# Half-height transpositions and a swapped order of projections in a linear-attention step

## The chip, the cores and the metric

The kernel runs on one core of one Trainium2 chip. The metric is the device time of one execution in microseconds (us). The engines are called as in the profile: PE is the matrix engine (PEld its weight loads), DVE, ACT and POOL are the vector, scalar and GpSimd engines, SP issues DMAs.

## What is computed

Three layers follow one another. The first is a linear attention over 8 batches, 8 heads, 576 positions and a head dimension of 64:

```python
def phi(x):
    proj = np.einsum('bhsd,df->bhsf', x, w_phi)
    proj = proj - np.max(np.abs(proj), axis=-1, keepdims=True)
    return np.concatenate([np.exp(proj), np.exp(-proj)], axis=-1)
q_p, k_p = (phi(q), phi(k))
kv = np.einsum('bhsf,bhsd->bhfd', k_p, v)
z = np.sum(k_p, axis=2)
num = np.einsum('bhsf,bhfd->bhsd', q_p, kv)
den = np.einsum('bhsf,bhf->bhs', q_p, z)[..., None] + 1e-06
```

Its output `num / den` is laid out as [batch, position, 512]. The second layer gates a 512x512 product with a causal convolution of five taps and a sigmoid and multiplies by a second 512x512 matrix. The third adds the real part of a two-dimensional Fourier transform, normalises, and adds a feed-forward block of width 2048 with ReLU. The change touches the first layer alone.

## The kernel before, in words

The attention works on 16 units (a pair of batches times a pair of heads, `NU`), and each unit has 1152 positions, in nine chunks of 128. A step takes three chunks (`CH = 3`), so that there are 48 steps (`TOT`). `run_attention` (line 1327) is a software pipeline written out by hand: turn `st` of its loop emits stages that belong to different steps, and under `manual_schedule` each engine carries them out in the order in which they are emitted. In one turn that order is:

- `emit_KV` (line 282) of step st-2: sums phi(k) times v over the positions. It uses tiles of 128 rows by 64 columns, two side by side. A step of the middle third of a unit has four pieces here and the others three, and it does two of them ahead of `emit_num`. When half a unit is summed, ACT copies the sums out (`kvT`); there is one PSUM buffer for them (`ps_kv`).
- `emit_num` (line 318) of step st-4: phi(q) times kv, in the same tiles of 128 by 64, into `nm`.
- `emit_Y` (line 264) of step st-1 for the keys (w = 0): DVE takes the largest absolute value of each row (line 268, `m`) and subtracts it (line 269, `y`). Then `emit_kE`, two exponentials on ACT. Then `emit_Y` for the queries (w = 1).
- `emit_XT` (line 343) of step st-5: three PE transpositions of 128x128 of the attention's output `xs`, into the PSUM tile that is also the keys' projection buffer (tag `pj0`). `emit_xT` (line 350): DVE copies the result out.
- `emit_X` (line 333) of step st-4: DVE divides num by den, from `nm` into `xs`.
- `emit_yT` (line 304) of step st-2: six PE transpositions of 128x128 of the queries' `y`, into the PSUM tile `tr`. `emit_qE` (line 312): two exponentials on ACT from there.
- `emit_P` (line 254) of step st, for the keys and then for the queries: projections of 64 rows by 128 columns, six for each, the two heads in the two halves of the rows. An f32 product is two instructions in the trace, so that there are 24 records for a step. The PSUM pool `ps_pj` (line 215) has one buffer for each tag, `pj0` for the keys and `pj1` for the queries.

All eight PSUM banks are taken. Between these stages the loop spreads the conversion of weights from 64 bits (`convert`, line 118: ACT lines 143, 147, 149 and POOL lines 144 to 151) and the copies of tables.

The last steps' remaining stages (`note_tail`, line 1292) and the two other layers are put in order by a planner, `place_ops`, from costs that stand in the code; the costs noted there for `emit_yT`, `emit_XT` and `emit_xT` are the same in both kernels.

Of the kernel before, what the change touches and what calls it, by code (L numbers as in the profile page):

```python
# [9 lines left out]
F32 = mybir.dt.float32  # L10
# [5 lines left out]
ACTF = mybir.ActivationFunctionType  # L16
# [5 lines left out]
NB, NH, S, D, F = 8, 8, 576, 64, 128  # L22
# [45 lines left out]
def attention_moe_mixer_kernel(  # L68
# [18 lines left out]
    nc = tc.nc  # L87
    pe, act, vec, gps = (Issue(x) for x in (nc.tensor, nc.scalar, nc.vector, nc.gpsimd))
    mm = pe.matmul

    def pool(stack, name, bufs, space=None, side=None):
        kw = {} if space is None else {"space": space}
        if side is not None:
            kw["side"] = side
        if space is not DRAM:
            kw["reuse_waits"] = "tile"
        return stack.enter_context(tc.tile_pool(name=name, bufs=bufs, **kw))
# [71 lines left out]
    ident = base.tile([128, 128], F32, name="ident")  # L169
# [22 lines left out]
    NG, CH = 3, 3  # L192
    HALVES = (slice(0, 64), slice(64, 128))
# [23 lines left out]
    qe_p = pool(att, "qe", 3)  # L217
# [14 lines left out]
    qE = {}  # L232
# [3 lines left out]
    xT = {}  # L236
# [14 lines left out]
    def chunks(t):  # L251
        return t[:, :, 0:CH * F].rearrange("p h (c f) -> p h c f", f=F)
# [11 lines left out]
    def emit_Y(i, w):  # L264
        pv = chunks(pj.pop((i, w)))
        m = sm_p.tile([128, 2, CH], F32, tag=f"m{w}", name="m")
        y = y_p.tile([128, 2, CH, F], F32, tag=f"y{w}", name="y")
        nc.vector.tensor_reduce(out=m, in_=pv, axis=AX.X, op=ALU.max, apply_absolute_value=True)  # L268
        nc.vector.tensor_tensor(out=y, in0=pv, in1=m.unsqueeze(3).to_broadcast([128, 2, CH, F]), op=ALU.subtract)  # L269
        yq[i, w] = y  # L270

    def emit_kE(i):
        y = yq.pop((i, 0))
        e = e_p.tile([128, 2, 2, CH, F], F32, tag="e", name="ke")
        nc.scalar.activation(out=e[:, 0], in_=y, func=ACTF.Exp)
        nc.scalar.activation(out=e[:, 1], in_=y, func=ACTF.Exp, scale=-1.0)
        kE[i] = e
# [4 lines left out]
    def emit_KV(i, part):  # L282
        u, g = divmod(i, NG)
        tv = raw[u][1]
        e = kE[i]
        for slot, j in KV_PARTS[g][part]:
            b = slot // 5
            if slot % 5 == 0:
                kvps[u, b] = ps_kv.tile([128, 4, 66], F32, tag="kv", name="kv")
            t = kvps[u, b]  # L290
            for h in range(2):
                for a in range(2):
                    w = 2 * h + a
                    for p in HALVES:
                        mm(t[p, w, :], e[:, a, h, j, p], tv[:, h, slot, :],
                           start=slot % 5 == 0 and w == 0, stop=slot % 5 == 4 and w == 3, skip_group_check=True)
            if slot % 5 == 4:
                if b == 0:
                    kvT[u] = sm_p.tile([128, 4, 2, 65], F32, tag="kvT", name="kvT")
                act.activation(out=kvT[u][:, :, b, :], in_=kvps.pop((u, b))[:, :, 0:65], func=ACTF.Copy)  # L300
        if part == len(KV_PARTS[g]) - 1:
            kE.pop(i)

    def emit_yT(i):
        y = yq.pop((i, 1))
        t = ps_tr.tile([128, 2, 512], F32, tag="tr", name="yt")
        for h in range(2):
            for j in range(CH):
                nc.tensor.transpose(t[:, h, j * F:(j + 1) * F], y[:, h, j, :], ident)  # L309
        yq[i, 2] = t  # L310

    def emit_qE(i, a):
        if a == 0:
            qE[i] = qe_p.tile([128, 2, 2, CH, F], F32, tag="qe", name="qe")
        t = yq[i, 2] if a == 0 else yq.pop((i, 2))
        act.activation(out=qE[i][:, a], in_=chunks(t), func=ACTF.Exp, scale=(1.0, -1.0)[a])

    def emit_num(i):
        u, g = divmod(i, NG)
        e = qE.pop(i)  # L320
        kt = kvT[u]
        nm[i] = t = ps_nm.tile([128, 2 * CH, 66], F32, tag="nm", name="nm")
        for j in range(CH):
            c = CH * g + j
            for h in range(2):
                for a in range(2):
                    for b, p in enumerate(HALVES):
                        if c != 4:
                            b = 0 if c < 4 else 1
                        mm(t[p, 2 * j + h, 0:65], e[:, a, h, j, p], kt[:, 2 * h + a, b, :],  # L330
                           start=(a == 0), stop=(a == 1))

    def emit_X(i):
# [9 lines left out]
    def emit_XT(i, space, tag):  # L343
        x = xs.pop(i)
        t = space.tile([128, 2, 512], F32, tag=tag, name="xt")
        for j in range(CH):
            nc.tensor.transpose(t[:, 0, j * F:(j + 1) * F], x[:, j].rearrange("p h d -> p (h d)"), ident)  # L347
        xs[i, 1] = t

    def emit_xT(i):  # L350
        t = xs.pop((i, 1))
        xT[i] = xT_p.tile([128, CH * F], F32, tag="xT", name="xT")
        vec.tensor_copy(out=xT[i], in_=t[:, 0, 0:CH * F])

    def x_parts(i):
        u, g = divmod(i, NG)
# [7 lines left out]
    def put_x(i):  # L364
        for b, o, k in x_parts(i):
            nc.sync.dma_start(out=o, in_=xT[i][:, k])
        xT.pop(i)
# [122 lines left out]
    def tap_steps():  # L490
        t, acc = late["xf", 0], late["sg", 0]
        act.activation(out=acc, in_=shifted(t, 0, 4), func=ACTF.Copy, scale=cw[:, 0, 4:5])
        for k in range(4):
            vec.scalar_tensor_tensor(
                out=acc, in0=shifted(t, 0, k), scalar=cw[:, 0, k:k + 1], in1=acc, op0=ALU.mult, op1=ALU.add
            )
            yield
# [829 lines left out]
    def run_attention():  # L1327
        lead = ((0, 1), (2, 0), (2, 1), (3, 0), (5, 0))
        todo = {}
        tap0 = tap_steps()  # L1330
        for i in range(len(pieces)):
            for l, slot in lead:
                todo.setdefault((i * (X_AT - 2 - lead[-1][0]) // (len(pieces) - 1) + l, slot), []).append(pieces[i])
        n_t = 2 * len(tables)
        did_t = 0
        with tc.manual_schedule():
            for st in range(TOT + 1):
                u, g = divmod(st, NG)

                def at(lag):  # L1340
                    return 0 <= st - lag < TOT

                two = at(2) and (st - 2) % NG == 1
                if two:
                    emit_KV(st - 2, 0)
                if at(4):
                    emit_num(st - 4)
                if at(6):
                    put_x(st - 6)
                if at(1):  # L1350
                    emit_Y(st - 1, 0)
                    emit_kE(st - 1)
                if at(2):
                    emit_KV(st - 2, int(two))
                for c in todo.get((st, 0), ()):
                    next(c)
                if at(1):
                    emit_Y(st - 1, 1)
                if at(5):
                    emit_XT(st - 5, ps_pj, "pj0")  # L1360
                    emit_xT(st - 5)
                if at(4):
                    emit_X(st - 4)
                if at(2):
                    emit_yT(st - 2)
                    for a in range(2):
                        emit_qE(st - 2, a)
                if at(0):
                    for w in range(2):
                        emit_P(st, w)  # L1370
                for c in todo.get((st, 1), ()):
                    next(c)
                for _ in range(2 * (TOT - 2 <= st < TOT)):
                    next(tap0)
                if g == 0 and u + 1 < NU:
                    load_kq(u + 1)
                if g == 2 and u + 1 < NU:
                    load_v(u + 1)
                while did_t < n_t and did_t * (X_AT - 5) < (st - 3) * n_t:
                    next(tables[did_t // 2])  # L1380
                    did_t += 1
                if st == X_AT:
                    assert did_t == n_t
                    load_x(0)
                    load_x(1)
                    for i in range(2):
                        late["sg", i] = P["g"].tile([128, 2, HS], F32, tag="acc", name="acc")
                if st in (X_AT + 2, X_AT + 3):
                    for i in range(2):
                        split_x(2 * (st - X_AT - 2) + i)  # L1390
            put_x(TOT - 5)
            note_mix()
            note_mlp()
            place_ops()
# [115 lines left out]
```

## Time and profile before

| | |
|---|---|
| time, median of 3 runs | 1330.14 us (1323.65 to 1333.59) |
| the profiled execution | 1323.75 us |
| its span | 1322.0 us |
| PE busy | 1288.3 us, 97% |
| PEld busy | 1186.2 us, 90% |
| DVE busy | 1151.7 us, 87% |
| ACT busy | 907.0 us, 69% |
| POOL busy | 771.1 us, 58% |

The span runs from the first to the last instruction of the program; the time holds 1.75 us more around it. Busy shares are means over stages that have different limits, so a stage is read from its own stretch of the timeline. The attention loop takes about the first 290 us. Some 41 of its 48 steps repeat one of two patterns with small differences, so one step of each stands for many.

### The profile page before, as it was taken

Reading aid. Unit: us, or ns where it says so; the run is one execution under the profiler, and the core shown is the slowest. Engines: PE = TensorE matmul, PEld = TensorE weight load, DVE = VectorE, ACT = ScalarE, POOL = GpSimd, SP = SyncE. Lnnn points to the kernel's source line nnn. Section 1 sums busy time; section 2 is a strip of 40 time slices with the busy share of each in tenths; the row PEclk is TensorE's granted clock in tenths of the full one; section 3 lists DMA queues with packets and bytes.
Section 4 is the critical chain, followed back from the end, with each engine's and each line's share of the span. In section 5 each row is a group of like instructions: output and inputs, shape, how many; then the busy total and the mean of one; then the engine's idle time right before and its main releaser. Section 6 shows DMA issues by size and latency. Waiting matters only on the chain.

```text
span 1322.0 us, 30500 instructions
## 1 busy us (share of the span) xinstructions
PE 1288.3 (97%) x11952; PEld 1186.2 (90%) x11952; DVE 1151.7 (87%) x1790; ACT 907.0 (69%) x1698; POOL 771.1 (58%) x641
## 2 busy tenths in 40 slices
PE   8999999988999998999999999999999999999998
PEld 7988888987999998998888888888888888889997
DVE  6888888889999999778999998988989898888885
ACT  7888897654656646466876687767677676776662
POOL 5787786213567676264654855597558855583321
PEclk9999999999999998999999999999999999999999
DMA  7597987613343442427433653357333743345322
GB/s 290 199 328 262 322 293 255 233 65 129 132 164 104 164 149 81 169 78 267 139 101 102 209 174 104 103 157 217 108 104 110 238 131 100 104 153 175 106 84 89
DMA packets 134444, 214.61 MB, mean 162 GB/s; under 512 B 17046, under 2 KB 92054, under 8 KB 134300
## 3 DMA queue, kind: packets, MB, share of 16 engines
q1 hardware_dynamic: 129840, 203.05, 46.3%
q10 hardware_dynamic: 4460, 9.62, 2.0%
q8 instruction: 93, 1.52, 0.5%
q14 instruction: 51, 0.42, 0.1%
HBM read 165.63 MB, written 46.99 MB: 161 GB/s over the span
## 4 chain that ended last, share of the span: by engine, by line
PE 90%; DVE 5%; ACT 3%; issue 1%; DMA 1%; SPq 0%; POOL 0%; DVEq 0%; ACTq 0%
PE x L64 15%; PE cx L64 15%; PE ps L64 14%; PE cy L64 11%; PE y L64 8%; PE val L64 7%; PE kv L64 5%; PE pj L64 5%; PE nm L64 4%; PE z L64 4%; PE yt L309 2%; PE xt L347 1%; DVE acc L64 1%; ACT qe L64 1%; DMA tab<-in_seq_tab_dram 0%
## 5 line engine op out<-in xcount | busy, mean ns | idle before, releaser
L64 POOL TENSOR_TENSOR r<-r 128x256 fp32r<-128x256 f32 (+1 forms) x301 | 292.5, 988 | 246.7 <-ACT r L64 226.1
L64 ACT ACTIVATE r<-r 128x256 fp32r<-128x256 f32 (+1 forms) x420 | 195.3, 487 | 57.6 <-DMA r<-s_scr 53.9
L64 PE MATMUL x<-un,r 128*128 128x462 f32 (+1 forms) x960 | 222.9, 373 | 2.2 <-ACT c L64 1.4
L64 PE MATMUL cx<-h,r 128*128 128x462 f32 (+1 forms) x960 | 213.9, 371 | 1.1 <-DVE acc L64 1.1
L64 PEld LDWEIGHTS x<-un,r 128*128 128x128 f32 x960 | 181.1, 189 | 24.1 <-DVE c L64 2.0
L64 PEld LDWEIGHTS cx<-h,r 128*128 128x128 f32 x960 | 180.3, 188 | 22.1 <-DVE acc L64 1.9
L64 PE MATMUL cy<-h,r 128*128 128x462 f32 (+1 forms) x720 | 160.2, 371 | 0.0
L64 PEld LDWEIGHTS cy<-h,r 128*128 128x128 f32 x720 | 135.4, 188 | 15.3
L64 PE MATMUL val<-xh,wv 128*128 128x290 f32 x768 | 116.8, 300 | 7.0 <-DVE gs L64 3.3
L64 PEld LDWEIGHTS val<-xh,wv 128*128 128x128 f32 x768 | 107.4, 190 | 9.6 <-DVE gs L64 4.0
L64 PE MATMUL y<-un,r 128*128 128x462 f32 (+1 forms) x480 | 114.1, 373 | 0.0
L64 DVE SCALAR_TENSOR_TENSOR acc<-xf,cw,acc 128x576 f32<-128x576 f32 x128 | 105.7, 829 | 6.9 <-ACT acc L64 6.1
L64 PE MATMUL ps<-ge,wo 128*128 128x290 f32 x768 | 108.9, 298 | 1.9 <-DVE A L64 1.9
L64 PEld LDWEIGHTS ps<-ge,wo 128*128 128x128 f32 x768 | 105.5, 190 | 2.3 <-DVE A L64 2.1
L268 DVE TENSOR_REDUCE m<-pj 128x6 f32<-128x768 f32 x96 | 91.4, 952 | 16.0 <-PE pj L64 15.3
L64 PEld LDWEIGHTS y<-un,r 128*128 128x128 f32 x480 | 90.4, 189 | 10.9 <-DVE h L64 0.3
L64 DVE TENSOR_TENSOR acc<-cx,acc 128x924 f32<-128x924 f32 (+1 forms) x80 | 88.9, 1111 | 10.1 <-PE cx L64 8.7
L269 DVE TENSOR_TENSOR y<-pj,m 128x768 f32<-128x768 f32 x96 | 91.9, 958 | 6.4
L64 PE MATMUL kv<-vraw,ke 128*64 128x66 f32 x2560 | 87.6, 223 | 2.4 <-ACT kvT L64 2.1
L64 PE MATMUL pj<-wp,kqraw 64*128 64x128 f32 x1152 | 81.4, 289 | 6.5 <-DMA kqraw<-in_k_dram 4.2
L64 PEld LDWEIGHTS pj<-wp,kqraw 64*128 64x128 f32 x1152 | 71.5, 194 | 18.0 <-DVE xT L64 10.2
L64 ACT ACTIVATE h<-z 128x462 fp32r<-128x462 f32 (+1 forms) x120 | 66.3, 553 | 29.0 <-DVE z L64 26.1
(170 smaller groups left out, 2729.2 us busy)
## 6 DMA issues: line engine op xcount, KB each, us to landing
r<-s_scr SPq DMA_DIRECT2D x280, 128.0 KB, 2.3
r<-s_scr SPq DMA_DIRECT2D x140, 256.0 KB, 2.6
raw<-in_w_ch_dram SPq DMA_DIRECT2D x16, 1024.0 KB, 5.1
vraw<-in_v_dram SPq DMA_DIRECT2D x16, 660.0 KB, 6.9
xf<-x_scr SPq DMA_DIRECT2D x8, 1152.0 KB, 6.4
u_scr<-u ACTq DMA_DIRECT2D x8, 1152.0 KB, 4.8
kqraw<-in_k_dram SPq DMA_DIRECT2D x15, 576.0 KB, 7.1
kqraw<-in_q_dram SPq DMA_DIRECT2D x15, 576.0 KB, 8.1
```

Source lines behind the costliest of these rows:

```text
L64: return lambda *a, **k: f(*(resolve(x) for x in a), **{n: resolve(x) for n, x in k.items()})
L268: nc.vector.tensor_reduce(out=m, in_=pv, axis=AX.X, op=ALU.max, apply_absolute_value=True)
L269: nc.vector.tensor_tensor(out=y, in0=pv, in1=m.unsqueeze(3).to_broadcast([128, 2, CH, F]), op=ALU.subtract)
L309: nc.tensor.transpose(t[:, h, j * F:(j + 1) * F], y[:, h, j, :], ident)
L347: nc.tensor.transpose(t[:, 0, j * F:(j + 1) * F], x[:, j].rearrange("p h d -> p (h d)"), ident)
```

## The change

`emit_yT` and `emit_XT` transpose 64 rows at a time instead of 128. Rows 0 to 63 of a chunk go through one row tile of PE and rows 64 to 127 through the other; each piece has 64 rows, 128 columns of data and a 64x64 identity as the moving operand, and the two halves land in two PSUM banks. So there are 12 transpositions for `yT` and 6 for `XT` in a step, instead of 6 and 3. The layout of `qE`, the reads of `emit_num` and the copy `emit_xT` follow the new order of the halves. In `run_attention` the queries are projected before the keys.

```diff
@@ emit_yT
         for h in range(2):
             for j in range(CH):
-                nc.tensor.transpose(t[:, h, j * F:(j + 1) * F], y[:, h, j, :], ident)
+                for r, p in enumerate(HALVES):
+                    nc.tensor.transpose(t[:, r, (CH * h + j) * 64:(CH * h + j + 1) * 64], y[p, h, j, :], ident[p, p])
@@ emit_qE
-            qE[i] = qe_p.tile([128, 2, 2, CH, F], F32, tag="qe", name="qe")
+            qE[i] = qe_p.tile([128, 2, 2, 2, CH, 64], F32, tag="qe", name="qe")
         t = yq[i, 2] if a == 0 else yq.pop((i, 2))
-        act.activation(out=qE[i][:, a], in_=chunks(t), func=ACTF.Exp, scale=(1.0, -1.0)[a])
+        act.activation(out=qE[i][:, a].rearrange("p r h c s -> p r (h c s)"), in_=t[:, :, 0:CH * F], func=ACTF.Exp, scale=(1.0, -1.0)[a])
@@ emit_num
-                    for b, p in enumerate(HALVES):
-                        if c != 4:
-                            b = 0 if c < 4 else 1
-                        mm(t[p, 2 * j + h, 0:65], e[:, a, h, j, p], kt[:, 2 * h + a, b, :],
+                    for r, p in enumerate(HALVES):
+                        b = r if c == 4 else int(c > 4)
+                        mm(t[p, 2 * j + h, 0:65], e[:, a, r, h, j, :], kt[:, 2 * h + a, b, :],
                            start=(a == 0), stop=(a == 1))
@@ emit_XT
         for j in range(CH):
-            nc.tensor.transpose(t[:, 0, j * F:(j + 1) * F], x[:, j].rearrange("p h d -> p (h d)"), ident)
+            for r, p in enumerate(HALVES):
+                nc.tensor.transpose(t[:, r, 64 * j:64 * j + 64], x[p, j].rearrange("p h d -> p (h d)"), ident[p, p])
@@ emit_xT
-        vec.tensor_copy(out=xT[i], in_=t[:, 0, 0:CH * F])
+        vec.tensor_copy(
+            out=xT[i].rearrange("p (c r s) -> p r c s", r=2, s=64), in_=t[:, :, 0:64 * CH].rearrange("p r (c s) -> p r c s", s=64),
+        )
@@ run_attention
                 if at(0):
-                    for w in range(2):
+                    for w in (1, 0):
                         emit_P(st, w)
```

## Rows read from the trace of the kernel before

**Rows 1.** The page: the chain that ended last, share of the span by engine.

```profile
PE 90%; DVE 5%; ACT 3%; issue 1%; DMA 1%; SPq 0%; POOL 0%; DVEq 0%; ACTq 0%
```

**Rows 2.** Windows: us, busy PE, PEld, DVE, ACT, POOL, PE clock, DMA share, GB/s.

```profile
92.00:147.00 55.00, 52.95 (x1206) 48.74 (x1204) 46.02 (x72) 48.19 (x62) 44.73 (x22) 1.00 0.83 304
...
320.00:1322.00 1002.00, 987.12 (x5418) 908.23 (x5416) 885.50 (x1365) 661.50 (x1376) 581.25 (x536) 0.99 0.43 137
```

**Rows 3.** Timeline, PE in a plain step: start us, us, what [idle before <-releaser].

```profile
152.41 1.61 PE L64 MATMUL pj<-wp,kqraw 64*128 64x128 f32 x24
...
153.95 1.62 PE L64 MATMUL nm<-kvT,qe 128*64 128x65 f32 x48
...
156.90 0.55 PE L347 MATMUL xt<-ident,xs 128*128 128x128 f32 x3
...
157.28 0.82 PE L309 MATMUL yt<-ident,y 128*128 128x128 f32 x6
...
158.09 1.42 PEld L64 LDWEIGHTS pj<-wp,kqraw 64*128 64x128 f32 x24 [0.23 <-DVE xT L64]
```

**Rows 4.** Timeline, DVE in the same step.

```profile
153.40 0.96 DVE L268 TENSOR_REDUCE m<-pj 128x6 f32<-128x768 f32 x1 [0.15 <-PE pj L64]
...
156.31 0.96 DVE L269 TENSOR_TENSOR y<-pj,m 128x768 f32<-128x768 f32 x1
...
157.48 0.56 DVE L64 COPY xT<-xt 128x384 f32<-128x384 f32 x1 [0.21 <-PE xt L347]
...
158.37 0.56 DVE L339 TENSOR_TENSOR xs<-nm,r 128x384 f32<-128x384 f32 x1
...
159.08 0.96 DVE L268 TENSOR_REDUCE m<-pj 128x6 f32<-128x768 f32 x1 [0.15 <-PE pj L64]
```

**Rows 5.** Timeline, the next step, with four pieces of KV.

```profile
163.05 0.55 PE L347 MATMUL xt<-ident,xs 128*128 128x128 f32 x3
...
163.64 0.56 DVE L64 COPY xT<-xt 128x384 f32<-128x384 f32 x1 [0.68 <-PE xt L347]
...
165.23 0.96 DVE L268 TENSOR_REDUCE m<-pj 128x6 f32<-128x768 f32 x1
```

**Rows 6.** Timeline, the attention's first steps.

```profile
4.24 3.08 PE L64 MATMUL pj<-wp,kqraw 64*128 64x128 f32 x24 [4.24 <-DMA kqraw<-in_k_dram]
...
6.09 0.96 DVE L268 TENSOR_REDUCE m<-pj 128x6 f32<-128x768 f32 x1 [5.04 <-PE pj L64]
...
8.94 0.96 DVE L269 TENSOR_TENSOR y<-pj,m 128x768 f32<-128x768 f32 x1
...
10.04 1.65 PE L64 MATMUL pj<-wp,kqraw 64*128 64x128 f32 x12 [0.20 <-DVE y L269]
...
25.53 0.96 DVE L268 TENSOR_REDUCE m<-pj 128x6 f32<-128x768 f32 x1 [0.53 <-PE pj L64]
```

**Rows 7.** Timeline, DVE: the keys' maximum 41 steps after the last of rows 6.

```profile
273.45 0.96 DVE L268 TENSOR_REDUCE m<-pj 128x6 f32<-128x768 f32 x1 [0.15 <-PE pj L64]
```

**Rows 8.** PE by form: count, busy us, mean ns of one, idle before.

```profile
L64 PE MATMUL nm<-kvT,qe 128*64 128x65 f32 x2304 | 78.1, 223 | 3.9 <-issue 2.7 <-DVE xs L339 1.1
...
L309 PE MATMUL yt<-ident,y 128*128 128x128 f32 x288 | 40.2, 276 | 1.6 <-ACT qe L64 1.6
```

**Rows 9.** PEld by form, the same columns.

```profile
L64 PEld LDWEIGHTS kv<-vraw,ke 128*64 128x64 f32 x2560 | 80.7, 138 | 5.4 <-ACT kvT L64 2.5 <-issue 0.9
...
L64 PEld LDWEIGHTS pj<-wp,kqraw 64*128 64x128 f32 x1152 | 71.5, 194 | 18.0 <-DVE xT L64 10.2 <-issue 6.0 <-PE pj L64 1.6
...
L309 PEld LDWEIGHTS yt<-ident,y 128*128 128x128 f32 x288 | 33.4, 143 | 2.0 <-ACT qe L64 1.8
```

**Rows 10.** Timeline, PEld: a stall inside a plain step.

```profile
100.99 0.14 PEld L64 LDWEIGHTS nm<-kvT,qe 128*64 128x64 f32 x2 [1.27 <-issue]
```

**Rows 11.** Timeline, PEld: a step whose projections wait for no semaphore.

```profile
18.44 0.64 PEld L309 LDWEIGHTS yt<-ident,y 128*128 128x128 f32 x6
19.24 1.42 PEld L64 LDWEIGHTS pj<-wp,kqraw 64*128 64x128 f32 x24 [0.16 <-issue]
```

## The prediction

> **What bounds the kernel now.** I read the chain of waits by engine first: PE holds 90% of it [rows 1]. After 320 us PE is busy for 987 of 1002 us [rows 2]; the change does not touch that part, so it moves as a block with the attention's end. The rest of the question is the attention's 48 steps, read from the timeline of single steps.
>
> From the keys' maximum to the next one a plain step takes 159.08 - 153.40 = 5.68 us [rows 4]; the next step, with four pieces of KV, takes 165.23 - 159.08 = 6.15 us [rows 4, 5]. Every third step is of the second kind. From step 4 to step 45 (41 steps, 14 of the second kind) 273.45 - 25.53 = 247.9 us pass [rows 6, 7]. 27 x 5.68 + 14 x 6.15 = 239.5, so 8.4 us are stalls of single steps, such as 1.27 us of PE's issue [rows 10].
>
> In the plain step three things close the loop. PE starts P at 152.41, starts XT at 156.90 (4.49 us later: P, num, KV), transposes until about 158.0, and then waits 0.23 us for DVE's copy xT, because the keys' projection reuses the buffer that XT wrote [rows 3]. DVE has waited 0.21 us for XT, copies, and finishes xs; then it waits 0.15 us for the keys' projection [rows 4]. So PE's chain runs P, num, KV, XT, copy, P, with yT partly under the copy. In the step with four pieces DVE waits 0.68 us for XT [rows 5], so that PE's chain alone sets it. ACT is no bound yet: 48.19 of 55 us [rows 2], about 5.3 us for a mean step of 6.05 us (247.9 / 41).
>
> **The change part by part.** *The transpositions.* Now six take 0.82 us, the last one 0.28 of it: 0.109 us apiece [rows 3, 8]. Durations of f32 products rise from 223 ns at 65 moving columns to 276 at 128 [rows 8], 0.84 ns a column, so a transposition of 128 columns is about paced by its moving columns: 0.107 us. A piece of the change has 64 moving columns, 0.054 us by the same slope, and nothing excludes that its load still costs as much as for a whole one. The trace shows no transposition in row tiles, so I bound a pair of pieces, one per row tile. Below: num's pairs, also two tiles with 64 columns loaded and 65 moving, come every (1.62 - 0.22) / 24 = 0.058 us [rows 3, 8]; less than 0.054 is excluded by the slope. Above: 0.109, a whole transposition, if the load sets the pace; and 0.218 if besides the two tiles take turns. For tiles side by side speak the projections, whose 24 records in 64-row tiles take 1.61 us, (1.61 - 0.27) / 12 = 0.112 for two records of 128 columns each [rows 3]. For a cheap load speaks that a transposition's load of 128 columns takes 143 ns, near the 138 of a 64-column load and not the 194 of the projections' 128 columns [rows 9]. I take 0.058. XT and yT then take 0.06 (first load) + 9 x 0.058 = 0.58 us. PE's own chain becomes 4.49 + 0.58 = 5.07 us in a plain step and 163.05 - 158.09 + 0.58 = 5.54 in the other [rows 3, 5].
>
> The Trainium skill (TensorE: Matmul & The Clock Gate, LDWEIGHTS) says a load takes its columns divided by 1.2 GHz, whatever the rows. Halving the rows would then save nothing. The 143 against 194 ns above contradict it for transpositions; no run here shows it for 64 rows. It is the first rival below.
>
> *The order of P.* The queries' half no longer waits for the copy xT, which hides under it. It has a wait of its own: `pj1` has one buffer, and its last reader is DVE's subtraction `y` of the queries in the same turn. That ends at 156.31 + 0.96 = 157.27, 3.87 us after the keys' maximum began [rows 4]. Behind the waiting load stand, on PE, the keys' projection and then num and KV of the next turn; DVE's next maximum waits for the keys' projection, now the second half. The new loop is: 3.87; a release of 0.05 (copy's end 158.04 to load 158.09); from P's start to the maximum 159.08 - 158.09 = 0.99 with six pairs; and six more pairs at 0.112, 0.67. Sum 5.58 us [rows 3, 4]. Before, this loop was not the longest. DVE's own work, 3.87 + (158.93 - 157.48) + 0.05 = 5.37, lies below it. So a plain step takes 5.58 (0.10 less) and a four-piece step max(5.58, 5.54) = 5.58 (0.57 less). Over 41 steps: 27 x 0.10 + 14 x 0.57 = 10.7 us.
>
> PE now idles up to 5.58 - 5.07 = 0.51 us in a plain step, so a stall inside one is swallowed up to that. Three plain steps have stalls of more than half a us, like that of [rows 10]; that gives 1.5 us. The four-piece steps swallow almost nothing.
>
> ACT's 5.3 us a step must now fit into some 5.7 with stalls. Its copy kvT sits between two pieces of KV, and in a four-piece step PE has no slack for a late one. My estimate is 0.3 us in half of those 14 steps, 2 us given back; ends 0 and 5 us.
>
> *The first four steps* lose. Before, the keys' projection of a step needs only the keys' subtraction, and the first steps overlap. With the queries first, (a) the first maximum comes after all 24 records: 4.24 + 3.08 + 0.05 = 7.37, not 6.09; (b) step 1's projections start only after the queries' subtraction, 9.90 - 6.09 = 3.81 later plus 0.14, and take 3.08 (these early ones are slow: twelve take 1.65): 7.37 + 3.95 + 3.08 + 0.05 = 14.45; (c) then three steps at 5.58: 31.2, where the trace has 25.53 [rows 6]. Cost 5.6 us, ends 4 and 7.
>
> *At nothing.* qE: as many elements from two banks as before. num: as many records, each a run of 64 columns as now. The copy xT now writes runs of 64: the product xs, with runs of 64 out of 66, takes 0.56 us for 384 elements as the copy does [rows 4]. If it took 0.3 us more it would still lie under the queries' projection; twice its price would make DVE's loop 5.93 and cost 14 us. The nine further transpositions of a step issue while PE waits; if they bring one or two more stalls like [rows 10], 1 to 3 us. The swap moves only matrix instructions: no DMA, and nothing on SP's or POOL's queue. The planner's order is the same.
>
> By the Trainium skill (TensorEngine Tiling, Key Properties) a change of tiling mode drains PE. The trace agrees: 0.16 us without a semaphore between yT and P [rows 11]. The change ends that one, as transpositions and projections share a shape. My 5.58 holds no gain from it, since P waits for DVE there; had the drain stayed, a four-piece step would be 5.70 and 1.7 us would be lost.
>
> **The sum.** -10.7 - 1.5 + 2.0 + 5.6 = -4.6 us. The profiled execution took 1323.75 us (span 1322.0), which gives 1319.2. It lay at the low end of the three runs; from their median, 1330.1 - 4.6 = 1325.5. All times below are by the median.
>
> **The rivals.**
>
> *A half costs a load as much as a whole* (0.109 a pair). PE's chains: 4.49 + 0.06 + 0.98 = 5.53 and 6.00. Plain steps still 5.58; the others win 0.15 only: 2.7 + 2.1 - 5.6 = -0.8 of gain, 1330.9. Chance 0.14. For it: the column count is unchanged. Against it: [rows 9].
>
> *Slower: the two row tiles take turns* (0.218 a pair). Chains 6.51 and 6.98, 41 x 0.83 + 5.6 = 39.6 us more, 1369.7. The place is PE between KV and P; the change loses from about 0.102 a pair, where 2.7 + 14 x (6.15 - 5.02 - 9p) equals the start's 5.6, and over 1% from 0.146. Against it: the projections run side by side in the same tiles [rows 3]. Chance 0.06.
>
> *ACT becomes the pace.* Its 5.3 us and its waits for y and yT add up to a step of about today's 5.68 for every kind: 14 x 0.47 - 5.6 = 1.0 us gained, 1329.1. For it: a share of 0.88 already [rows 2]. Against it: kE and qE are needed a whole turn later. Chance 0.15.
>
> *Faster: the queries' projection is not held by the subtraction*, so that DVE paces plain steps at 5.37, PE the others at 5.54, and the start loses nothing: 27 x 0.31 + 14 x 0.61 + 0.9 of stalls = 17.8 us, 1312.3. Against it: in the second step the queries' projection did wait for DVE's y [rows 6]. Chance 0.10.
>
> **How the numbers follow.** The forecast has 0.55; its own range, from the ends of its start, ACT and issue terms, is 1318 to 1332. The whole range, 1310 to 1336, takes in all but the slower rival and the tails of what measurement adds. 1% (13.3 us) is about what a measurement of this kernel tells from no change. Faster by more: the last rival's 0.10 and 0.08 of the forecast, 0.18. Slower by more: 0.06 and 0.01. Within: 0.75.
>
> **What would show it.** Right: plain and four-piece steps alike near 5.58 us; the projections' load waiting for DVE's y in place of xT; DVE waiting for XT no longer, and some 0.25 us for the projections; yT's twelve in about 0.6 us; the fifth keys' maximum at about 31 us. Wrong: yT still near 0.8 us or above (the load, or tiles in turn); steps at 5.4 (no hold by y); kvT waits in many steps (ACT); a fifth maximum near 26 us.

## The result, and the profile after

The changed kernel takes 1333.74 us (median of 22 runs, 1324.77 to 1338.64), the kernel before 1325.04 us in the same sessions (22 runs, 1318.71 to 1333.59). The ratio is 1.0056 with a 95% interval of 1.0041 to 1.0070: by the ratio 7.4 us slower (the medians lie 8.7 us apart). The forecast was 4.6 us faster. The profiled execution of the changed kernel took 1338.05 us (span 1336.3), 14.3 us more than that of the kernel before. It was the second slowest of its 22, so it shows where the time goes better than how much.

Most of the pattern forecast for a step is there. First the timeline of a plain step of the changed kernel, from one keys' maximum to the next (PE, PEld and DVE; start us, us, what [idle before <-releaser]), which answers to [rows 3, 4]:

```profile
107.30 0.96 DVE L268 TENSOR_REDUCE m<-pj 128x6 f32<-128x768 f32 x1 [0.36 <-PE pj L64]
...
110.14 0.40 PE L348 MATMUL xt<-ident,xs 64*128 64x64 f32 x6
...
110.37 0.54 PE L310 MATMUL yt<-ident,y 64*128 64x64 f32 x12
111.10 0.55 DVE L64 COPY xT<-xt 128x384 f32<-128x384 f32 x1
111.23 1.42 PEld L64 LDWEIGHTS pj<-wp,kqraw 64*128 64x128 f32 x24 [0.46 <-DVE y L269]
...
112.89 0.96 DVE L268 TENSOR_REDUCE m<-pj 128x6 f32<-128x768 f32 x1 [0.36 <-PE pj L64]
```

The step takes 112.89 - 107.30 = 5.59 us, where 5.58 was worked out. DVE starts the copy xT without a wait, the projections' load waits for DVE's `y`, and DVE waits 0.36 us for the projections. Twelve half transpositions take 0.54 us, six whole ones took 0.82.

The start is as forecast too, but a little dearer. The fifth keys' maximum comes at 31.96 us (31.2 was forecast, 25.53 it was [rows 6]):

```profile
6.05 2.08 PE L64 MATMUL pj<-wp,kqraw 64*128 64x128 f32 x16 [1.09 <-DMA kqraw<-in_q_dram]
...
8.17 0.96 DVE L268 TENSOR_REDUCE m<-pj 128x6 f32<-128x768 f32 x1 [7.12 <-PE pj L64]
...
12.13 2.93 PE L64 MATMUL pj<-wp,kqraw 64*128 64x128 f32 x24 [4.00 <-DVE y L269]
...
31.96 0.96 DVE L268 TENSOR_REDUCE m<-pj 128x6 f32<-128x768 f32 x1 [0.91 <-PE pj L64]
```

What was not forecast stands in the 41 steps between the fifth and the forty-sixth keys' maximum. I call this stretch the loop. The windows of it, of the kernel before and then of the changed one (us, busy PE, PEld, DVE, ACT, POOL, PE clock, DMA share, GB/s):

```profile
25.53:273.45 247.92, 242.16 (x5517) 223.55 (x5515) 209.71 (x330) 204.33 (x267) 165.66 (x84) 1.00 0.75 264
```

```profile
31.96:286.72 254.76, 228.78 (x5886) 216.41 (x5888) 207.55 (x331) 202.68 (x267) 164.70 (x83) 0.97 0.73 257
```

PE has 13.4 us less to do, and the loop is 6.8 us longer: PE idles 26.0 us in it, where it idled 5.8. At 5.59 us a step the loop would take 229.2 us, so 25.6 us are stalls; before they were 8.4. Of the profiled 14.3 us, the start is +6.4 (31.96 - 25.53), the undisturbed steps are -10.3 (229.2 - 239.5), the stalls +17.2, and what follows the loop +1.0 (1049.6 against 1048.5 us).

The groups of weight loads in the loop say whose stalls they are (count, busy us, mean ns | idle before us <-releasers). Before:

```profile
L64 PEld LDWEIGHTS kv<-vraw,ke 128*64 128x64 f32 x2192 | 69.1, 138 | 4.1 <-ACT kvT L64 1.8 <-issue 0.5
L64 PEld LDWEIGHTS nm<-kvT,qe 128*64 128x64 f32 x1968 | 61.4, 138 | 6.6 <-issue 3.2
L64 PEld LDWEIGHTS pj<-wp,kqraw 64*128 64x128 f32 x986 | 58.6, 187 | 10.9 <-DVE xT L64 9.5 <-issue 1.3
```

After:

```profile
L64 PEld LDWEIGHTS kv<-vraw,ke 128*64 128x64 f32 x2192 | 71.3, 140 | 11.8 <-issue 8.4 <-ACT kvT L64 1.6
L64 PEld LDWEIGHTS nm<-kvT,qe 128*64 128x64 f32 x1974 | 64.1, 141 | 10.3 <-issue 7.2
L64 PEld LDWEIGHTS pj<-wp,kqraw 64*128 64x128 f32 x984 | 61.4, 194 | 12.3 <-DVE y L269 7.0 <-issue 5.3
L310 PEld LDWEIGHTS yt<-ident,y 64*128 64x128 f32 x492 | 19.1, 141 | 1.1 <-issue 1.1
```

"issue" is time for which no semaphore accounts. It was 0.5 + 3.2 + 1.3 = 5.0 us; it is 8.4 + 7.2 + 5.3 + 1.1 = 22.0. These waits fall anywhere: in the middle of KV, of num, of P, of yT. They share another thing. The timeline of the weight loads from one such wait to the next, in the changed kernel:

```profile
146.03 0.60 PEld L64 LDWEIGHTS kv<-vraw,ke 128*64 128x64 f32 x17 [1.80 <-issue]
146.70 0.26 PEld L348 LDWEIGHTS xt<-ident,xs 64*128 64x128 f32 x6
146.89 0.46 PEld L310 LDWEIGHTS yt<-ident,y 64*128 64x128 f32 x12
147.26 1.43 PEld L64 LDWEIGHTS pj<-wp,kqraw 64*128 64x128 f32 x24
148.81 1.02 PEld L64 LDWEIGHTS kv<-vraw,ke 128*64 128x64 f32 x32
149.73 1.19 PEld L64 LDWEIGHTS nm<-kvT,qe 128*64 128x64 f32 x37
152.60 0.37 PEld L64 LDWEIGHTS nm<-kvT,qe 128*64 128x64 f32 x10 [1.68 <-issue]
```

17 + 6 + 12 + 24 + 32 + 37 = 128 loads, and each load has its product: 256 instructions lie between the two waits. Counted from PE's first record, semaphore instructions included, every one of the 16 such waits of over 0.25 us in the loop stands at place 193 or 194 of a run of 256, and so do the 5 of the kernel before and all those of the experiments. The page lists packets of a kind of their own, the instructions (DMA queue: packets, MB, share of the 16 engines):

```profile
q8 instruction: 97, 1.59, 0.5%
```

1.59 MB in 97 packets are 16.4 KB each: 256 instructions of 64 bytes. So PE had run out of instructions and waited for the next piece. The DMA view around the wait before 146.03 (first 137.0 to 143.7 us, then 143.7 to 144.7; columns as in the last) shows one piece, and when it comes:

```profile
q1 hardware_dynamic: 596, 2.15, 91.5%
...
q1 hardware_dynamic: 341, 0.35, 99.6%
q8 instruction: 1, 0.02, 5.5%
```

For 6.7 us no piece comes while data hold the DMA engines for nine tenths of the time. Then one comes between 143.7 and 144.7, PE stops at 146.03 - 1.80 = 144.23, and it goes on 1.3 us or more after the piece.

The trace times every piece like this. At each of the 16 waits PE goes on 1.2 to 1.5 us after its piece has landed; it passes none of the 30 other such places of the loop earlier than 1.3 us after. A piece is about 1.0 us on its way. What varies is when it sets out, counted from PE's passing of the place before: 3.2 to 4.9 us for the 16 late pieces (3.9 in the mean), with the DMA engines busy with data for 0.94 of that time or more; 1.6 us in the mean for the others, with a share of 0.68. So a mean wait is 3.9 + 1.0 + 1.4 less the 5.0 us in which PE uses 256 instructions, 1.3 us. In the kernel before pieces set out late as well, 16 of 44 later than 2.6 us against 20 of 46 here; but PE takes 5.5 us for 256 instructions there, and only 5 came too late.

By the Trainium skill (Runtime: NRT & Kernel Launch, Instruction fetch mechanics) the instructions come in blocks of 16 KiB, 256 of them, which the trace confirms (16.4 KB). The same section of the Trainium skill adds that the cost of crossing such a boundary is "mostly hidden". Here the crossings cost PE 22 us of 255.

### The profile page after: what moved, and what is told of

Read it like the earlier page. It is cut to its first block, busy times and chain, and to the rows that moved or that the text cites. A ratio compares the mean times of both kernels' runs of the same rounds, so it can differ in the third digit from the quotient of the medians.

```text
span 1336.3 us, 31374 instructions
## 1 busy us (share of the span) xinstructions
PE 1274.5 (95%) x12384; PEld 1178.8 (88%) x12384; DVE 1148.1 (86%) x1790; ACT 907.9 (68%) x1698; POOL 771.9 (58%) x641
## 3 DMA queue, kind: packets, MB, share of 16 engines
q8 instruction: 97, 1.59, 0.5%
## 4 chain that ended last, share of the span: by engine, by line
PE 85%; DVE 10%; issue 2%; ACT 2%; DMA 1%; SPq 0%; POOL 0%; DVEq 0%
PE x L64 15%; PE cx L64 15%; PE ps L64 13%; PE cy L64 11%; PE y L64 8%; PE val L64 7%; PE pj L64 5%; PE z L64 4%; PE kv L64 4%; DVE y L269 3%; PE nm L64 3%; DVE m L268 3%; DVE acc L64 1%; PE yt L310 1%; PE xt L348 1%
## 5 line engine op out<-in xcount | busy, mean ns | idle before, releaser
L64 PE MATMUL kv<-vraw,ke 128*64 128x66 f32 x2560 | 91.2, 226 | 9.7 <-issue 7.5
L64 PEld LDWEIGHTS pj<-wp,kqraw 64*128 64x128 f32 x1152 | 74.9, 201 | 26.0 <-issue 11.1
L64 PEld LDWEIGHTS kv<-vraw,ke 128*64 128x64 f32 x2560 | 83.9, 141 | 13.4 <-issue 8.8
```

Of the source, the lines that this page charges most:

```text
L64: return lambda *a, **k: f(*(resolve(x) for x in a), **{n: resolve(x) for n, x in k.items()})
```

## The experiments

Theory 1: what is lost in the loop is PE's waits for pieces of its instruction stream, because the change makes PE use them up faster (18 more instructions in a step, and shorter steps) while data transfers delay their arrival. Theory 2: the order of the projections is to blame, since PE now stands before P until DVE releases it.

**The order alone** (`swap_only`): the kernel before with one line changed.

```diff
-                    for w in range(2):
+                    for w in (1, 0):
                         emit_P(st, w)
```

> The kernel before with the queries projected first, and whole 128-row transpositions. Theory 1 (PE reads its instructions in pieces of 256; more instructions in a shorter step make the pieces come late): the instruction stream is that of before, so PE's idle time put down to issue at every 256th instruction stays near the 7.5 us of before (6 places) and not the 23.8 us of after (17 places); the fifth keys' maximum comes at about 31 to 32 us, steps take about 5.70 and 6.2 us; 6 to 8 us slower than before, ratio about 1.005. Theory 2 (it is the order: PE, held by the wait for the queries' subtraction, can't read ahead): the places stay near 17 and the idle time above 18 us, 18 to 22 us slower, ratio about 1.016.

(The expectation counts the whole attention, with one wait behind the loop in each kernel; the results count the loop.) Ratio to before 1.0007 (0.9990 to 1.0024). Steps take 5.62 and 6.09 us, and the fifth maximum comes at 31.96. Eight places of issue idle, 4.8 us. The weight loads of KV, num and P in its loop:

```profile
L64 PEld LDWEIGHTS kv<-vraw,ke 128*64 128x64 f32 x2192 | 69.0, 138 | 5.7 <-ACT kvT L64 3.3 <-issue 0.7
L64 PEld LDWEIGHTS nm<-kvT,qe 128*64 128x64 f32 x1974 | 61.9, 138 | 5.9 <-issue 2.4
L64 PEld LDWEIGHTS pj<-wp,kqraw 64*128 64x128 f32 x984 | 58.6, 188 | 8.6 <-issue 4.7 <-DVE y L269 3.9
```

Of the 4.7 us before P, 1.7 stand at three of the eight places. The other 3.0 are 18 waits of 0.17 us behind the whole transpositions, none at such a place: the kind of [rows 11], which the changed kernel has no more. Theory 2 falls: the wait for `y` is there and the long issue waits are not. The kernel came out about 1 us slower, not 6 to 8. The steps gained 2.5 us in the loop; what else makes up for the start is not shown.

**The halves alone** (`half_only`): the changed kernel with the keys first.

```diff
-                    for w in (1, 0):
+                    for w in range(2):
                         emit_P(st, w)
```

> The changed kernel with the keys projected first again: half transpositions alone. Theory 1 (instructions): plain steps about 5.54 us, four-piece steps about 6.0 us, the fifth keys' maximum at about 25.5 us as before, and issue idle time at every 256th instruction 15 to 25 us: 5.7 us won and some 14 lost, 6 to 10 us slower than before, ratio about 1.006. Theory 2 (order): issue idle time near 7 us as before, 5 us faster, ratio about 0.996.

Ratio 1.0034 (1.0017 to 1.0051), about 4.5 us slower, less than expected. Undisturbed steps 5.54 and 6.01 us, the fifth maximum at 24.77. 17 places, 16.1 us:

```profile
L64 PEld LDWEIGHTS kv<-vraw,ke 128*64 128x64 f32 x2192 | 70.3, 138 | 8.8 <-issue 5.9 <-ACT kvT L64 1.1
L64 PEld LDWEIGHTS nm<-kvT,qe 128*64 128x64 f32 x1968 | 62.2, 138 | 10.2 <-issue 6.8
L64 PEld LDWEIGHTS pj<-wp,kqraw 64*128 64x128 f32 x986 | 59.0, 188 | 19.5 <-DVE xT L64 16.8 <-issue 2.6
```

The stalls go with the half transpositions, although each step became shorter by only 0.14 us.

**The start** (`late_swap`): the changed kernel, with the keys first in the first four turns.

```diff
-                    for w in (1, 0):
+                    for w in ((0, 1) if st < 4 else (1, 0)):
                         emit_P(st, w)
```

> The changed kernel, but the first four turns project the keys first. If the start is a separate cost of the order: the fifth keys' maximum back at about 26 us, 5 to 6 us less than the changed kernel, ratio to before about 1.001. If what is saved at the start is given back later: as the changed kernel, 1.005. Both theories on issue say that the idle time at every 256th instruction stays near that of after (15 to 25 us).

Ratio 1.0015 (0.9997 to 1.0034), the fifth maximum at 25.36 us. The median is 1328.42 against 1333.74 in other sessions, 5.3 us less, and the ratios differ by as much: the start is a cost of its own and comes back. Issue idle in the loop stays, 22.8 us in 19 places.

**Both transpositions ahead of the last KV** (`xtyt_early`), keys first, so that no step waits for the copy.

```diff
                 if at(2):
+                if at(5):
+                    emit_XT(st - 5, ps_pj, "pj0")
+                if at(2):
+                    emit_yT(st - 2)
+                if at(2):
                     emit_KV(st - 2, int(two))
...
                 if at(5):
-                    emit_XT(st - 5, ps_pj, "pj0")
                     emit_xT(st - 5)
...
                 if at(2):
-                    emit_yT(st - 2)
                     for a in range(2):
                         emit_qE(st - 2, a)
```

> Half transpositions, keys projected first, and both transpositions of a turn moved ahead of its last KV on PE, so that DVE's copy xT waits for nothing and the keys' projection follows the copy. Steps of both kinds about 5.45 to 5.55 us, the start as before: 13 us won in the loop. Theory 1 (instructions): 15 us of issue idle time more than before eat that, ratio 0.998 to 1.003. Theory 2 (order): idle time near 7 us, 12 us faster, ratio about 0.991.

Ratio 1.0030 (1.0011 to 1.0049). Plain steps fall to 5.41 us, the shortest of all, and the four-piece steps to 5.81 where nothing disturbs them, not 5.5. The loop takes 257.6 us, 18.2 of them issue idle. A faster step gave a slower kernel.

**Halves in a third of the steps** (`half_third`): `late_swap`, with half transpositions only where a step has four pieces of KV.

```diff
+                if i % NG != 1:
+                    nc.tensor.transpose(t[:, h, j * F:(j + 1) * F], y[:, h, j, :], ident)
+                    continue
                 for r, p in enumerate(HALVES):
                     nc.tensor.transpose(t[:, r, (CH * h + j) * 64:(CH * h + j + 1) * 64], y[p, h, j, :], ident[p, p])
```

(XT, the copy and the reads of num in the same way.)

> The changed order from the fifth turn on, and half transpositions only in the steps with four pieces of KV (a third of them): 6 records more a step on average instead of 18. Theory 1 (instructions): plain steps 5.62 as with the order alone, four-piece steps about 5.6, start as before, issue idle time 4 to 9 us in the loop: some 5 to 8 us faster than before, ratio 0.994 to 0.996. If the stalls come with half transpositions as such: issue idle near 15 us and a ratio of 1.000 or more.

Ratio 0.9991 (0.9975 to 1.0008), no difference. The undisturbed steps are as expected, 5.62 and 5.58 us, but the fifth maximum comes at 27.08 us, and the issue idle time is 11.7 us in 12 places, not 4 to 9. That lies between the 7.5 us of `order_late` below, the same order without halves, and the 22.8 of `late_swap`: a third of the added instructions brings about a third of the added stalls.

**The instructions without their use** (`padded`): the kernel before with nine small transpositions more in a step.

```diff
+        for k in range(9):
+            p = HALVES[k % 2]
+            nc.tensor.transpose(t[:, k % 2, 448:512], y[p, 0, 0, :], ident[p, p])
         yq[i, 2] = t
```

> The kernel before with nine additional 64-row transpositions a step whose result nobody reads (18 records, as many as the change adds); whole transpositions and the old order stay. Theory 1 (the count of PE's instructions): 12 to 18 places of issue idle time at a 256th instruction in the loop and 12 to 22 us of it, though no step became shorter. Rival (it takes the shorter step or the layout of the changed kernel): 5 to 8 places and about 5 us, as before.

1340.8 us in one run. Steps grow to 5.93 and 6.40 us, 0.17 of it a wait in each step among the transpositions, where their shape changes, not at a 256th instruction. Still 12 places stand in the loop, 8.8 us of idle time. The number of places is as theory 1 has it, the time is below it: between the two.

**Without the loads of weights** (`before_noload`, `after_noload`), in both kernels:

```diff
-        raw = P["xf"].tile([128, 1024, 2], I32, tag="xf", name="raw64")[:, 0:n]
+        if i >= 7:
+            raw = held[i % 2]
+        else:
+            raw = held[i % 2] = P["xf"].tile([128, 1024, 2], I32, tag="xf", name="raw64")[:, 0:n]
         raw_k = raw.rearrange("p n t -> p (n t)").rearrange("p (k f) -> p k f", k=shape[0])
-        if shape[0] == 8:
+        if i >= 7:
+            pass
+        elif shape[0] == 8:
             nc.sync.dma_start(out=raw_k.rearrange("p (o q) f -> p o (q f)", o=2), in_=src)
...
+    held = {}
```

> The kernel before without 16 of its loads of 64-bit weights: every feed-forward piece converts what the loads for the first pieces left, so the output is not the reference's. If instruction pieces come late because data transfers hold the DMA engines: issue idle time in the loop under 1.5 us, and the loop from the fifth maximum near 241 us. If they are late for a reason of PE's own: about 5 us of idle time as before.

> The changed kernel without the same 16 loads (again not the reference's output). If data transfers hold the instruction pieces up: issue idle time in the loop falls from 21 us to under 5, steps of both kinds stay at 5.59, and the loop takes 230 to 236 us, shorter than that of the kernel before without the loads by 6 us or more. If not: issue idle time stays at 15 us or more.

The loads left out are 14 of the 16 of the feed-forward weights, not 16 as the expectation says. The kernel before has one place of 0.33 us left, and its loop takes 242.5 us:

```profile
L64 PEld LDWEIGHTS kv<-vraw,ke 128*64 128x64 f32 x2192 | 68.6, 138 | 3.9 <-ACT kvT L64 2.2
L64 PEld LDWEIGHTS nm<-kvT,qe 128*64 128x64 f32 x1968 | 60.8, 138 | 3.3
L64 PEld LDWEIGHTS pj<-wp,kqraw 64*128 64x128 f32 x986 | 58.4, 187 | 9.8 <-DVE xT L64 9.5 <-issue 0.3
```

The changed one has ten places, 9.0 us, and a loop of 241.3 us:

```profile
L64 PEld LDWEIGHTS kv<-vraw,ke 128*64 128x64 f32 x2192 | 69.9, 138 | 7.4 <-ACT kvT L64 3.3 <-issue 2.3
L64 PEld LDWEIGHTS nm<-kvT,qe 128*64 128x64 f32 x1973 | 61.9, 138 | 6.0 <-issue 2.6
L64 PEld LDWEIGHTS pj<-wp,kqraw 64*128 64x128 f32 x984 | 59.9, 190 | 10.8 <-DVE y L275 8.4 <-issue 2.2
L316 PEld LDWEIGHTS yt<-ident,y 64*128 64x128 f32 x492 | 19.1, 141 | 2.1 <-issue 2.1
```

With the data traffic down, 13.5 us came back in the changed kernel's loop and 5.4 in the other's; its loop is now the shorter one, by 1.2 us and not the 6 forecast. The whole kernels take 1324.1 us (changed) and 1321.7 us in one run each: the changed one still carries its start. That data transfers delay the pieces is shown. Nine us are left, not the "under 5" forecast, and the loop did not get to 236 us, with 3.3 us of it a wait for ACT's kvT. The nine do not speak against data: transfers still fill 0.62 to 0.64 of the DMA engines' time (0.73 to 0.81 with the loads), and the ten late pieces set out 2.9 to 4.5 us after the place before, with the engines busy for 0.82 of that time or more.

**More time for each piece** (`after_slow`): the changed kernel with a further maximum on DVE in each turn.

```diff
                     emit_Y(st - 1, 1)
+                    mx2 = sm_p.tile([128, 2, CH], F32, tag="mx2", name="mx2")
+                    nc.vector.tensor_reduce(out=mx2, in_=yq[st - 1, 1], axis=AX.X, op=ALU.max, apply_absolute_value=True)
```

> The changed kernel with one more maximum on DVE a turn, between the queries' subtraction and the copy xT, whose result nobody reads: DVE's loop grows from 5.37 to about 6.25 and the step from 5.59 to about 6.3 us, with the same instructions on PE. If what counts is how long PE takes for a piece of 256 instructions (4.96 us in the changed kernel, 5.54 before): a piece takes about 5.6 us, issue idle time falls from 21 us to about 5, and the loop takes 262 to 268 us, against 254.8 now though 29 us of work on its path were added. If what counts is the number of instructions: issue idle time stays at 15 to 23 us and the loop takes 275 us or more.

Steps of 6.37 us; 12 places, 10.7 us of issue idle; the loop 270.0 us. The idle time halves with the same instructions, so the pace counts. But it stays at twice that of the kernel before, whose pieces last no longer: here 18 of 46 pieces set out later than 3.2 us after the place before, there 10 of 44. Why more are late here is not shown.

**The order alone, later** (`order_late`): the kernel before, queries first from the fifth turn on.

```diff
-                    for w in range(2):
+                    for w in ((0, 1) if st < 4 else (1, 0)):
                         emit_P(st, w)
```

> The kernel before, with the queries projected first from the fifth turn on and whole transpositions everywhere. If the start is a cost of its own and the halves' instructions the other: start as before (fifth keys' maximum at about 25.5 us), steps 5.62 and 6.09 as with the order alone, issue idle time in the loop about 5 us as before; the order alone came out 1 us slower than before with 5 to 6 us lost at the start, so 4 to 5 us faster than before, ratio 0.996 to 0.997. If the start's loss was hidden anyway: ratio near 1.000.

Ratio 0.9978 (0.9957 to 0.9999): about 3 us faster than the kernel before, by an interval that ends just under 1, and faster than the changed one. The profile does not show that gain: the execution it was taken from (1326.07 us) is slower than that of the kernel before, with the fifth maximum at 26.58 us, not 25.5, and eight places, 7.5 us. A plain step of it:

```profile
248.52 0.96 DVE L268 TENSOR_REDUCE m<-pj 128x6 f32<-128x768 f32 x1 [0.39 <-PE pj L64]
...
252.31 0.55 DVE L64 COPY xT<-xt 128x384 f32<-128x384 f32 x1
...
254.14 0.96 DVE L268 TENSOR_REDUCE m<-pj 128x6 f32<-128x768 f32 x1 [0.39 <-PE pj L64]
```

The step is 5.62 us with whole transpositions: the swap alone brings 0.06 of the 0.09 us that a plain step of the changed kernel wins.

The loops side by side. "Piece" is the time in which PE uses 256 instructions in undisturbed steps: 256 x (27 plain + 14 four-piece steps) / PE's records in the loop, semaphore instructions included. "Places" and "issue idle" count PE's waits of over 0.25 us (the groups above hold the shorter ones too). Each row is one profiled execution.

| kernel | undisturbed steps us | piece us | places | issue idle us | loop us |
|---|---|---|---|---|---|
| before | 5.68, 6.15 | 5.54 | 5 | 5.0 | 247.9 |
| swap_only | 5.62, 6.09 | 5.47 | 8 | 4.8 | 247.0 |
| order_late | 5.62, 6.09 | 5.47 | 8 | 7.5 | 251.0 |
| padded | 5.93, 6.40 | 5.41 | 12 | 8.8 | 261.2 |
| half_third | 5.62, 5.58 | 5.19 | 12 | 11.7 | 250.8 |
| half_only | 5.54, 6.01 | 5.07 | 17 | 16.1 | 254.5 |
| after | 5.59, 5.59 | 4.96 | 16 | 21.5 | 254.8 |
| late_swap | 5.59, 5.59 | 4.96 | 19 | 22.8 | 251.9 |
| xtyt_early | 5.41, 5.81 | 4.93 | 14 | 18.2 | 257.6 |
| after_slow | 6.37, 6.37 | 5.65 | 12 | 10.7 | 270.0 |
| before_noload | 5.68, 6.15 | 5.54 | 1 | 0.3 | 242.5 |
| after_noload | 5.58, 5.58 | 4.95 | 10 | 9.0 | 241.3 |

Among the kernels with the same transfers the idle time rises, nearly in order, as the piece gets shorter; `after_slow` is the exception.

## Why the prediction was wrong

The sum was -10.7 - 1.5 + 2.0 + 5.6 = -4.6 us. That 1333.74 lies inside the stated 1310 to 1336 is luck: the range stood on a median of three runs, 1330.1, and 22 runs of the same kernel gave 1325.04.

**The loop's gain, -10.7, was right.** 27 plain steps of 5.59 and 14 four-piece steps of 5.59 are 10.3 us less than before. The pair of half transpositions cost about (0.54 - 0.225) / 5 = 0.063 us, taking the mean product of 225 ns and five spacings between six pairs; 0.058 was taken. The loop through the queries' subtraction set the pace, as worked out. The first and the slower rival (a half as dear as a whole; tiles in turn) are out by that number, and the faster one by the projections' load, which did wait for `y`.

**The start, +5.6, was right** within its ends: 6.4 us in the profile, 5.3 us by `late_swap`'s median. The difference to 5.6 in the profile is mostly the second part of the queries' load, for which PE waited 1.09 us.

**ACT's term, +2.0, was an estimate that hardly showed.** ACT did not become the pace, and KV's waits for kvT in the loop went from 1.8 to 1.6 us.

**The failed step is the term for further stalls of issue.** It stood under "at nothing": nine further transpositions issue while PE waits; "if they bring one or two more stalls", 1 to 3 us. In the loop issue idle rose from 5.0 to 22.0 us, and all stalls from 8.4 to 25.6, where the sum had them fall by 1.5. The prediction had a row of such a stall [rows 10] and took it for a thing that happens now and then. It asked neither after its period nor after what it waits for. It counted PE's time and not PE's instructions: 18 more in a step of 270 records, used up in a shorter time. The page had the instruction packets as a queue of their own, and the trace the 256 between waits.

**The same term explains the size.** In the profiled executions 17.2 us of stalls take the 10.3 us gained by the steps, and the start's 6.4 come on top. By the measured 7.4 us in place of the profiles' 14.3 the stalls would be some 10 us more than before, an estimate from the same terms. `half_only` (halves without the order) loses by stalls what its steps gain, and more; `order_late` (order without halves and without the start) wins, narrowly. What the change brings would need pieces that come in time.

That a late piece is the cause is shown: the waits stand 256 instructions apart and end 1.2 to 1.5 us after a piece has landed, the late pieces set out while data fill the DMA engines, the waits all but vanish in the kernel before when 14 loads go, and they follow the added instructions in `padded`, where nothing else was gained. By the times of the pieces the added instructions and the shorter step act through one number, the time that PE takes for 256 instructions (5.54 us before, 4.96 after). Open stays which pieces meet full DMA engines: each row of the table is one execution, and the scatter of issue idle time between executions was not measured. Open too is why a piece isn't asked for earlier. The trace does not show the asking; it shows that in no loop of the table a piece set out more than 0.9 us before PE passed the place before.

## What to carry to other kernels

Where an engine is busy nearly all the time, count its instructions as well as its time: splitting a product in two halves may cost the array nothing (here a pair took less than the whole) and still cost more than it saves if the instruction stream shares the DMA engines with heavy loads. In the trace, look at "issue" idle time first by its period: waits that stand 256 instructions apart are the instruction stream, whatever line they fall on. And price the first turns of a software pipeline apart: an order that helps the steady loop can hold up its start, and can be put in after it.

## What the runs showed of the hardware

A long wait for an instruction piece can be followed by a slower PE clock. In the changed kernel the wait of 1.87 us before 96.96 us was followed by a stretch at a lower granted clock (windows, 97 to 101 us; columns as above):

```profile
97.00:101.00 4.00, 4.00 (x66) 3.93 (x67) 1.38 (x4) 2.25 (x4) 3.92 (x2) 0.65 0.99 382
```

0.65 is a mean over the halved level, 1.2 GHz, and the full 2.4. PE's timeline there:

```profile
96.96 1.04 PE L64 MATMUL kv<-vraw,ke 128*64 128x66 f32 x28 [1.87 <-issue]
...
98.79 2.88 PE L64 MATMUL pj<-wp,kqraw 64*128 64x128 f32 x24
```

The projections take 2.88 us in place of 1.61 [rows 3], and that step took 9.17 us (keys' maximum at 92.54, the next at 101.71). The loop has three such stretches, from 98.2, 176.7 and 231.3 us, beside its three longest waits for a piece (2.0, 2.2 and 3.1 us before a load, ended at 96.96, 175.64 and 231.63); the kernel before has none in its loop. The clock's mean over the loop was 0.97, where it had been 1.00. That the wait brings the lower clock on was not tested: `half_only` has 16.1 us of such waits and no such stretch in its loop.

The load of a half transposition takes as long as that of a whole one (141 against 141 ns in the loop), and still the pair costs about 0.06 us in place of 0.109. The records show why: in the step at 110.13 us the two loads of a pair start 3 to 6 ns apart and the next pair 0.06 us later, so that loads in the two row tiles run side by side. The Trainium skill (TensorE: Matmul & The Clock Gate, LDWEIGHTS) has a load cost its columns whatever its rows. The equal durations agree with it; the price of a pair shows that for these transpositions the load's duration is not what is paid.
